# A retention recurrence and a multiplicative FFN on one core: w3 @ w_out multiplied once on the chip, the recurrence done chunk by chunk for all heads with head pairs padded to the full array, in a fixed instruction order

## The chip, the core and the metric

The kernel runs on one core of one Trainium2 chip. The metric is the device time of one execution in microseconds (us). Where a median is quoted it is that of the runs of one session; the kernel before was run beside every kernel of this study, in the same session and on the same chip as it (the sessions had different chips), and stayed at 430.7 to 433.3 us as a median. Engines are named as in the profile: PE is TensorE, PEld its weight loads, DVE is VectorE, ACT is ScalarE, POOL is GpSimd, SP is the engine that issues the DMAs here.

## The reference, cut to what matters

```python
# q, k, v: (4 batches, 8 heads, 768 steps, 64), float32
for t in range(S):
    state = gamma[h] * state + outer(k[:, :, t], v[:, :, t])
    y[:, :, t] = (1 / sqrt(D)) * (q[:, :, t] @ state)
x = y as (3072 tokens, 512)
a = x @ w1                  # 512 x 1024
b = x @ w2                  # 512 x 1024
h = (a * b) @ w3            # 1024 x 1024
return h @ w_out            # 1024 x 512
```

Two facts of it carry the change. Nothing stands between `@ w3` and `@ w_out`, so the two can be one matrix of 1024 x 512. And the decays `gamma` differ only by head, so chunks of 128 steps of all eight heads can be treated alike.

## The kernel before

Both kernels use the chunked form of the recurrence: within a chunk of 128 steps, masked scores times V; between chunks, a 64 x 64 state per head. All matmuls are in float16 with float32 sums. The kernel before takes one head of one batch after another. Its unit of work is one chunk of one head, and each unit uses the array in four shapes:

```python
def run_head(b, h, ffn_rate):            # for 32 heads, 6 chunks each
    for c in range(NCH + 2):             # three stages, one chunk apart
        # stage 3: YS[0:64] = V^T ATm + S^T tq ; K^T V for the state
        nc.tensor.matmul(YS[0:64], lhsT=V16[...], rhs=st["atm"], ...)          # 128*64
        nc.tensor.matmul(YS[0:64], lhsT=prev, rhs=st["tq"], ...)               # 64*64
        nc.tensor.matmul(YS[64:128, 0:64], lhsT=QgK[...], rhs=V16[...], ...)   # 128*64
        ...                              # copies to XT, new state, scaled state
        # stage 2: scores and mask
        nc.tensor.matmul(ATps, lhsT=st["tk"], rhs=st["tq"], ...)               # 64*128
        nc.vector.tensor_tensor(ATm, ATps, MASKT[h], MULT)
        # stage 1: one transpose of [q k]
        nc.tensor.transpose(Tps, QgK[...], ident16)                            # 128*128
        ...                              # copies tq (ScalarE), tk (VectorE)
        slot_filler()                    # pulls FFN units at a set rate
```

The FFN is a generator whose units are pulled between chunk steps. A tile of 512 tokens has 8 units of w1, 8 of w2 (four 512-column matmuls each), then the third layer, then 4 output units:

```python
for gb in range(8):
    psG = ps_g.tile([128, TB], FP, tag="psG")
    for f1b in range(8):
        nc.tensor.matmul(psG, lhsT=W3[f1b][:, gb*128:(gb+1)*128], rhs=HT[f1b], ...)
    gt = fsb.tile([128, TB], HP, tag=f"gt{gb}")
    nc.scalar.copy(gt, psG)
    yield
...
gpb = 28
quota = {0: 0, 1: 1 * gpb, 2: 3 * gpb, 3: 4 * gpb}   # FFN units to be done by the end of batch b
```

Of the kernel before, what the change touches and what calls it, by code (L numbers as in the profile page):

```python
# [9 lines left out]
FP = mybir.dt.float32  # L10
# [3 lines left out]
ADD = mybir.AluOpType.add  # L14


@with_exitstack
def kernel(
# [14 lines left out]
    NCH = S // C  # L33
    NTOK = B * S
    DM = 512
    DFF = 1024
    scale = 1.0 / math.sqrt(D)
# [3 lines left out]
    wstage = ctx.enter_context(tc.tile_pool(name="wstage", bufs=4))  # L41
    xpool = ctx.enter_context(tc.tile_pool(name="xpool", bufs=1))
    rsb = ctx.enter_context(tc.tile_pool(name="rsb", bufs=4))
    tpool = ctx.enter_context(tc.tile_pool(name="tpool", bufs=3))
    spool = ctx.enter_context(tc.tile_pool(name="spool", bufs=4))
    fsb = ctx.enter_context(tc.tile_pool(name="fsb", bufs=2))

    ps_r = ctx.enter_context(tc.tile_pool(name="ps_r", bufs=3, space=bass.MemoryType.PSUM))
    ps_a = ctx.enter_context(tc.tile_pool(name="ps_a", bufs=1, space=bass.MemoryType.PSUM))
    ps_b = ctx.enter_context(tc.tile_pool(name="ps_b", bufs=1, space=bass.MemoryType.PSUM))  # L50
    ps_g = ctx.enter_context(tc.tile_pool(name="ps_g", bufs=2, space=bass.MemoryType.PSUM))
    ps_o = ctx.enter_context(tc.tile_pool(name="ps_o", bufs=1, space=bass.MemoryType.PSUM))

    XT = [xpool.tile([128, NTOK], HP, name=f"xt{fb}") for fb in range(4)]

    heads = [(b, h) for b in range(B) for h in range(H)]

    def head_dma(b, h):
        QK = rsb.tile([128, NCH * 128], FP, tag=f"qk")
        V6 = rsb.tile([128, NCH * 64], FP, tag=f"v6")  # L60
        qk_view = QK[:, :].rearrange("p (c x) -> p c x", x=128)
        nc.sync.dma_start(
            qk_view[:, :, 0:64], q[b, h].rearrange("(c i) d -> i c d", c=NCH)
        )
        nc.sync.dma_start(
            qk_view[:, :, 64:128], k[b, h].rearrange("(c i) d -> i c d", c=NCH)
        )
        nc.sync.dma_start(
            V6[:, :].rearrange("p (c d) -> p c d", d=64),
            v[b, h].rearrange("(c i) d -> i c d", c=NCH),  # L70
        )
        return QK, V6

    dma_tiles = {}
    for h in range(H):
        dma_tiles[(0, h)] = head_dma(0, h)
# [4 lines left out]
    nc.scalar.copy(ident16[:, :], ident[:, :])  # L81

    iota64 = const.tile([128, 64], mybir.dt.int32, name="iota64")
    nc.gpsimd.iota(iota64[:, :], pattern=[[0, 64]], base=0, channel_multiplier=1)
    iotaf = const.tile([128, 64], FP, name="iotaf")
    nc.vector.tensor_copy(iotaf[:, :], iota64[:, :])

    SC = []
    MASKT = []
    GC = []  # L90
    for h in range(H):
        g = 1.0 - 2.0 ** (-5.0 - h)
        lg = math.log(g)
        sc_h = const.tile([128, 128], FP, name=f"sc{h}")
        bq = const.tile([128, 1], FP, name=f"bq{h}")
        nc.gpsimd.memset(bq[:, :], lg + math.log(scale))
        bk = const.tile([128, 1], FP, name=f"bk{h}")
        nc.gpsimd.memset(bk[:, :], (C - 1) * lg)
        nc.scalar.activation(sc_h[:, 0:64], iotaf[:, :], AF.Exp, bias=bq, scale=lg)
        nc.scalar.activation(sc_h[:, 64:128], iotaf[:, :], AF.Exp, bias=bk, scale=-lg)  # L100
        maskt_h = const.tile([128, 128], FP, name=f"maskt{h}")
        make_upper_triangular(nc, maskt_h[:, :], val=g ** (-C), diag=True)
        SC.append(sc_h)
        MASKT.append(maskt_h)
        GC.append(g**C)

    def load_weights(w_ap, nblk, ncol, name):
        tiles = []
        for i in range(nblk):
            stg = wstage.tile([128, ncol], FP, tag="wst", name=f"stg_{name}{i}")  # L110
            nc.sync.dma_start(stg[:, :], w_ap[i * 128 : (i + 1) * 128, :])
            w16 = wpool.tile([128, ncol], HP, name=f"{name}{i}")
            if i % 2 == 0:
                nc.vector.tensor_copy(w16[:, :], stg[:, :])  # L114
            else:
                nc.scalar.copy(w16[:, :], stg[:, :])  # L116
            tiles.append(w16)
        return tiles

    W1 = load_weights(moe_w1, 4, DFF, "w1")  # L120
    W2 = load_weights(moe_w2, 4, DFF, "w2")
    W3 = load_weights(moe_w3, 8, DFF, "w3")
    WO = load_weights(moe_w_out, 8, DM, "wo")

    TB = 512
    NTB = NTOK // TB

    def ffn_gen():
        pending = []

        def out_stage(tok0, GT):
            def run(tb):
                psO = ps_o.tile([128, DM], FP, tag="psO")
                for gb in range(8):
                    nc.tensor.matmul(  # L135
                        psO[:, :],
                        lhsT=GT[gb][:, tb * 128 : (tb + 1) * 128],
                        rhs=WO[gb][:, :],
                        start=(gb == 0),
                        stop=(gb == 7),  # L140
                    )
                osb = fsb.tile([128, DM], FP, tag="osb")
                nc.scalar.copy(osb[:, :], psO[:, :])  # L143
                nc.sync.dma_start(
                    out[tok0 + tb * 128 : tok0 + (tb + 1) * 128, :], osb[:, :]
                )
            return [(run, tb) for tb in range(TB // 128)]

        for t in range(NTB):
            tok0 = t * TB  # L150
            HT = []
            for f1b in range(8):
                psA = ps_a.tile([128, TB], FP, tag="psA")
                for fb in range(4):
                    nc.tensor.matmul(  # L155
                        psA[:, :],
                        lhsT=W1[fb][:, f1b * 128 : (f1b + 1) * 128],
                        rhs=XT[fb][:, tok0 : tok0 + TB],
                        start=(fb == 0),
                        stop=(fb == 3),  # L160
                    )
                pa = fsb.tile([128, TB], FP, tag="pa")
                nc.scalar.copy(pa[:, :], psA[:, :])  # L163
                yield
                psB = ps_b.tile([128, TB], FP, tag="psB")
                for fb in range(4):
                    nc.tensor.matmul(  # L167
                        psB[:, :],
                        lhsT=W2[fb][:, f1b * 128 : (f1b + 1) * 128],
                        rhs=XT[fb][:, tok0 : tok0 + TB],  # L170
                        start=(fb == 0),
                        stop=(fb == 3),
                    )
                ht = fsb.tile([128, TB], HP, tag=f"ht{f1b}", name=f"ht{t%2}_{f1b}")
                nc.vector.tensor_tensor(ht[:, :], pa[:, :], psB[:, :], MULT)  # L175
                HT.append(ht)
                yield
                if pending and f1b % 2 == 1:
                    fn, tb = pending.pop(0)
                    fn(tb)  # L180
                    yield
            GT = []
            for gb in range(8):
                psG = ps_g.tile([128, TB], FP, tag="psG")
                for f1b in range(8):
                    nc.tensor.matmul(  # L186
                        psG[:, :],
                        lhsT=W3[f1b][:, gb * 128 : (gb + 1) * 128],
                        rhs=HT[f1b][:, :],
                        start=(f1b == 0),  # L190
                        stop=(f1b == 7),
                    )
                gt = fsb.tile([128, TB], HP, tag=f"gt{gb}", name=f"gt{t%2}_{gb}")
                nc.scalar.copy(gt[:, :], psG[:, :])  # L194
                GT.append(gt)
                yield
                if pending and gb % 2 == 1:
                    fn, tb = pending.pop(0)
                    fn(tb)
                    yield  # L200
            while pending:
                fn, tb = pending.pop(0)
                fn(tb)
                yield
            pending = out_stage(tok0, GT)
        while pending:
            fn, tb = pending.pop(0)
            fn(tb)
            yield

    fgen = ffn_gen()
    ffn_done = [False]

    def pull_ffn(n):
        for _ in range(n):
            if ffn_done[0]:
                return
            try:
                next(fgen)
            except StopIteration:  # L220
                ffn_done[0] = True
                return

# [116 lines left out]
    while not ffn_done[0]:  # L340
        pull_ffn(1)
# [30 lines left out]
```

## Time and profile before

| | |
|---|---|
| time, median (range) | 431.19 us (430.96 to 431.57), 4 runs |
| profiled span | 429.0 us |
| PE busy | 392.2 us, 1888 matmuls and transposes |
| of these, third layer of the FFN | 384 matmuls |
| DVE / ACT / POOL busy | 216.4 / 175.2 / 36.0 us |

The page's rows of costliest groups give the line, engine, operation, tiles, shape and count; then the busy time in us and the mean of one instruction in ns; then the idle time ahead of them. The largest row is the third FFN layer:

```profile
L186 PE MATMUL psG<-ht,w 128*128 128x512 f16 x384 | 100.1, 381 | 0.0
```

The mean of 381 ns in this row is how long one matmul is in the pipe, and it overlaps with its neighbours. What a matmul costs TensorE is the distance from its start to the next start, 0.216 us for these. I use that distance throughout, and it is read from the timeline. The lines that show what bounds this kernel stand in the prediction.

### The profile page before, as it was taken

The numbers are of one execution on the slowest core, as the hardware profiler recorded it, in microseconds if no ns is written. First come the engines' busy times: TensorE is split into PE (matmuls) and PEld (weight loads), VectorE is DVE, ScalarE is ACT, GpSimd is POOL, SyncE is SP. The second block draws the span as 40 slices with busy tenths as digits, with TensorE's granted clock in tenths as the row PEclk, the third lists the DMA queues.
The fourth block names the chain that finished last, engine by engine and source line by source line (L and its number), as shares of the span: only waits on it lengthen the run. The fifth ranks groups of instructions, "written<-read, shape, count | busy, mean of one in ns | idle before, by whom it ended". The sixth has DMA issues, their size and how long they took to land.

```text
span 429.0 us, 6007 instructions
## 1 busy us (share of the span) xinstructions
PE 392.2 (91%) x1888; PEld 173.0 (40%) x1888; DVE 216.4 (50%) x829; ACT 175.2 (41%) x534; POOL 36.0 (8%) x71
## 2 busy tenths in 40 slices
PE   0677877799999989999999999999999999999995
PEld 0333333334444433444444444444444444444442
DVE  2666766658755565675565642566654453012100
ACT  5234465433444433444444334444444343233331
POOL 5211000010011120111111110111010000000000
PEclk9999999999999986999999999999999999999999
DMA  8971886795422342222223320201000001001102
GB/s 185 220 232 51 240 256 200 180 192 126 96 55 57 90 121 55 55 57 55 57 56 104 82 77 4 57 26 44 30 2 0 3 24 49 26 0 50 49 0 99
DMA packets 82209, 36.05 MB, mean 84 GB/s; under 512 B 76033, under 2 KB 76033, under 8 KB 82177
## 3 DMA queue, kind: packets, MB, share of 16 engines
q1 hardware_dynamic: 82176, 35.66, 32.7%
q8 instruction: 15, 0.25, 0.3%
q14 instruction: 18, 0.14, 0.1%
HBM read 29.36 MB, written 6.29 MB: 83 GB/s over the span
## 4 chain that ended last, share of the span: by engine, by line
PE 87%; DVE 5%; ACT 3%; issue 2%; DMA 2%; SPq 1%; DVEq 0%; ACTq 0%
PE psG L186 21%; PE psB L167 12%; PE psA L155 11%; PE psO L135 10%; PE R L264 8%; PE R L272 7%; PE R L306 7%; PE R L279 6%; PE R L321 5%; DVE ATm L314 2%; DMA stg_wo<-in_moe_w_out_dram 1%; DMA QK<-in_k_dram 1%; DVE S_new L292 1%; ACT osb L143 1%; ACT xt L286 1%
## 5 line engine op out<-in xcount | busy, mean ns | idle before, releaser
L186 PE MATMUL psG<-ht,w 128*128 128x512 f16 x384 | 100.1, 381 | 0.0
L286 ACT CAST xt<-R 64x128 f16<-64x128 f32 x192 | 49.5, 258 | 117.6 <-PE R L279 111.3
L314 DVE TENSOR_TENSOR ATm<-R,maskt 128x128 f16<-128x128 f32 x192 | 55.5, 291 | 73.5 <-PE R L306 70.0
L167 PE MATMUL psB<-xt,w 128*128 128x512 f16 x192 | 62.2, 395 | 0.2 <-ACT w L116 0.2
L326 ACT COPY tq<-R 64x128 f16<-64x128 f16 x192 | 48.8, 259 | 32.9 <-PE R L321 30.1
L155 PE MATMUL psA<-xt,w 128*128 128x512 f16 x192 | 58.5, 398 | 0.8 <-DVE w L114 0.5
L264 PE MATMUL R<-ATm,V 128*64 128x128 f16 x192 | 48.1, 253 | 10.0 <-DVE ATm L314 9.1
L321 PE MATMUL R<-ident,QgK 128*128 128x128 f16 x192 | 45.1, 242 | 11.6 <-DVE QgK L231 6.5
L229 POOL CAST V<-V 128x384 f16<-128x384 f32 x32 | 31.5, 984 | 277.9 <-PE R L279 229.3
L175 DVE TENSOR_TENSOR ht<-pa,psB 128x512 f16<-128x512 f32 x48 | 33.0, 687 | 43.0 <-PE psB L167 42.1
L135 PE MATMUL psO<-wo,gt 128*128 128x512 f16 x192 | 51.0, 380 | 2.4 <-ACT osb L143 2.3
L292 DVE TENSOR_TENSOR S_new<-R,ssc 64x64 f16<-64x64 f32 x160 | 36.1, 225 | 31.3 <-ACT xt L286 27.5
L306 PE MATMUL R<-tq,tk 64*128 64x128 f16 x192 | 45.0, 243 | 6.0 <-DVE tk L327 4.7
L327 DVE COPY tk<-R 64x128 f16<-64x128 f16 x192 | 42.1, 224 | 11.4 <-ACT tq L326 8.6
L186 PEld LDWEIGHTS <-w 128*128 128x128 f16 x384 | 33.6, 98 | 32.6
L194 ACT CAST gt<-psG 128x512 f16<-128x512 f32 x48 | 28.0, 585 | 39.3 <-PE psG L186 39.0
L264 PEld LDWEIGHTS <-V 128*64 128x64 f16 x192 | 21.3, 112 | 55.7 <-issue 47.3
L272 PE MATMUL R<-tq,S_new 64*64 64x128 f16 x160 | 41.6, 260 | 2.3 <-DVE S_new L292 0.8
L279 PE MATMUL R<-V,QgK 128*64 128x64 f16 x192 | 43.6, 229 | 0.0
L231 DVE TENSOR_TENSOR QgK<-QK,sc 128x768 f16<-128x768 f32 x32 | 30.5, 954 | 20.7 <-PE R L279 14.0
L163 ACT COPY pa<-psA 128x512 f32<-128x512 f32 x48 | 28.1, 585 | 30.2 <-PE psA L155 29.1
L272 PEld LDWEIGHTS <-S_new 64*64 64x64 f16 x160 | 17.4, 109 | 42.6 <-DVE S_new L292 15.4
(29 smaller groups left out, 189.8 us busy)
## 6 DMA issues: line engine op xcount, KB each, us to landing
stg_w<-in_moe_w_dram SPq DMA_DIRECT2D x16, 512.0 KB, 4.2
QK<-in_q_dram SPq DMA_DIRECT2D x32, 192.0 KB, 3.3
QK<-in_k_dram SPq DMA_DIRECT2D x32, 192.0 KB, 3.7
V<-in_v_dram SPq DMA_DIRECT2D x32, 192.0 KB, 3.4
out_dram<-osb SPq DMA_DIRECT2D x24, 256.0 KB, 2.0
stg_wo<-in_moe_w_out_dram SPq DMA_DIRECT2D x8, 256.0 KB, 2.8
```

The lines of the kernel that those rows point to most:

```text
L135: nc.tensor.matmul(psO[:, :], lhsT=GT[gb][:, tb * 128 : (tb + 1) * 128], rhs=WO[gb][:, :], start=(gb == 0), stop=(gb == 7),)
L155: nc.tensor.matmul(psA[:, :], lhsT=W1[fb][:, f1b * 128 : (f1b + 1) * 128], rhs=XT[fb][:, tok0 : tok0 + TB], start=(fb == 0), stop=(fb == 3),)
L167: nc.tensor.matmul(psB[:, :], lhsT=W2[fb][:, f1b * 128 : (f1b + 1) * 128], rhs=XT[fb][:, tok0 : tok0 + TB], start=(fb == 0), stop=(fb == 3),)
L186: nc.tensor.matmul(psG[:, :], lhsT=W3[f1b][:, gb * 128 : (gb + 1) * 128], rhs=HT[f1b][:, :], start=(f1b == 0), stop=(f1b == 7),)
L264: nc.tensor.matmul(YS[0:64], lhsT=V16[:, c3 * 64 : (c3 + 1) * 64], rhs=st["atm"][:, :], start=True, stop=(prev is None),)
L272: nc.tensor.matmul(YS[0:64], lhsT=prev[:, :], rhs=st["tq"][:, :], start=False, stop=True,)
L279: nc.tensor.matmul(YS[64:128, 0:64], lhsT=QgK[:, c3 * 128 + 64 : (c3 + 1) * 128], rhs=V16[:, c3 * 64 : (c3 + 1) * 64], start=True, stop=True,)
L286: nc.scalar.copy(XT[fb][r0 : r0 + 64, col0 + c3 * 128 : col0 + (c3 + 1) * 128], YS[0:64],)
L306: nc.tensor.matmul(ATps, lhsT=st["tk"][:, :], rhs=st["tq"][:, :], start=True, stop=True,)
L314: nc.vector.tensor_tensor(ATm[:, :], ATps, MASKT[h][:, :], MULT)
L321: nc.tensor.transpose(Tps, QgK[:, c * 128 : (c + 1) * 128], ident16[:, :])
L326: nc.scalar.copy(tq[:, :], Tps[0:64])
```

## The change

It has three parts. First, `w3 @ w_out` is multiplied once on the chip, which removes the third layer. Second, the recurrence takes one chunk of all 8 heads at a time. Two heads share the 128 rows of the array: q and V of the pair stand in tiles with zeros in the other head's half, so every matmul is 128*128. Third, the framework's scheduler is switched off (`manual_schedule`): each engine's instructions run in the order in which the program writes them. Intent: less work for TensorE, no changes of array shape, and few large instructions on the other engines.

```diff
+    ctx.enter_context(tc.manual_schedule())
...
+    def w3_transpose(f):                 # W3[f]: 128 rows of w3
+        ps = ps_t.tile([128, 1024], HP, tag="psT", name="psT")
+        for g in range(8):
+            nc.tensor.transpose(ps[:, g*128:(g+1)*128], W3[f][:, g*128:(g+1)*128], ident16[:, :])
+        t = att.tile([128, 1024], HP, tag="w3t", name="w3t")
+        nc.vector.tensor_copy(t[:, :], ps[:, :])
+    def w3_mm(f):
+        for g in range(8):
+            nc.tensor.matmul(ps[:, :], lhsT=t[:, g*128:(g+1)*128], rhs=WO[g][:, :], ...)
+        nc.scalar.copy(W3O[f][:, :], ps[:, :])
+    w3_transpose(0)
+    for f in range(8):
+        if f + 1 < 8:
+            w3_transpose(f + 1)
+        w3_mm(f)
...
+    def transposes(n):      # 4 of q, 4 of k; copies kT, qT (VectorE), qp twice (ScalarE)
+    def scores(n):          # 4 matmuls of 256 columns: lhsT=kT pair, rhs=qp padded; mask x2
+    def kv(n):              # 4 matmuls K^T V; state sum (VectorE) and its scaling (GpSimd)
+    def outputs(n):
+        for p in range(NP):
+            nc.tensor.matmul(ps[:, p, :], lhsT=vp[:, p, 0, :], rhs=am[:, p, 0, :], ...)
+            nc.tensor.matmul(ps[:, p, :], lhsT=vp[:, p, 1, :], rhs=am[:, p, 1, :], ...)
+            if c > 0:
+                nc.tensor.matmul(ps[:, p, :], lhsT=Tst[0][:, p, :], rhs=qT[:, p, :], ...)
...
-            for gb in range(8):          # the third layer, see above
...
+    for n in range(NSTEP):               # 24 steps
+        load_chunk(n + PRE)
+        ...                              # m FFN units for this step, in four parts
+        casts(n + 2)
+        transposes(n + 1)
+        pull(parts[0])
+        scores(n)
+        pull(parts[1])
+        t_new = kv(n)
+        pull(parts[2])
+        outputs(n)
+        pull(parts[3])
```

All weights go through six staging buffers. The loads are issued in this order: w_out and w3, chunks 0 and 1, w1 and w2, the other chunks.

## The prediction

> **What bounds the kernel now.** I read the page's head and its chain of waits first, then stretches of the span cut by stage, then the order of matmuls inside the longest stage.
>
> ```profile
> span 429.0 us, 6007 instructions
> PE 392.2 (91%) x1888; PEld 173.0 (40%) x1888; DVE 216.4 (50%) x829; ACT 175.2 (41%) x534; POOL 36.0 (8%) x71
> ...
> PE 87%; DVE 5%; ACT 3%; issue 2%; DMA 2%; SPq 1%; DVEq 0%; ACTq 0%
> ```
>
> TensorE holds 87% of the chain that ends last; VectorE and ScalarE are half idle. The stretches (span, then busy time with instructions of PE, PEld, DVE, ACT, POOL, then granted clock, DMA share, GB/s) show three stages:
>
> ```profile
> 0.00:83.00 83.00, 54.52 (x234) 25.80 (x235) 50.10 (x200) 38.39 (x124) 11.11 (x47) 1.00 0.74 195
> 83.00:90.00 7.00, 6.75 (x19) 1.84 (x18) 3.38 (x12) 2.20 (x6) 1.52 (x3) 1.00 1.20 219
> 90.00:360.00 270.00, 267.65 (x1351) 117.44 (x1351) 155.40 (x608) 113.57 (x368) 23.35 (x21) 0.98 0.24 58
> 360.00:429.00 69.00, 63.31 (x288) 27.95 (x286) 7.55 (x11) 21.06 (x36) 0.00 (x0) 0.99 0.10 39
> ```
>
> Up to 83 us almost only batch 0's recurrence runs; from 90 to 360 us recurrence and FFN are mixed; the rest is FFN alone. In the FFN-alone stretch, groups of four 512-column matmuls start at 385.97, 386.84 and 387.70 us: (387.70 - 385.97) / 8, one per 0.216 us. The same stretches for the recurrence's PSUM tile alone:
>
> ```profile
> 90.00:360.00 270.00, 126.86 (x693) 0.98 0.24 58
> ```
>
> The other 658 matmuls there are FFN ones: 658 x 0.216 = 142 us. That leaves 270 - 142 = 128 us for 693 small matmuls, 0.185 us each, although they stream only 64 or 128 columns (128/512 of 0.216 is 0.054). The timeline shows why (start, duration, line, shape; `128*64` is the part of the array used):
>
> ```profile
> 245.10 0.24 PE L264 MATMUL R<-ATm,V 128*64 128x128 f16 x1
> 245.27 0.24 PE L272 MATMUL R<-tq,S_new 64*64 64x128 f16 x1
> 245.44 0.22 PE L279 MATMUL R<-V,QgK 128*64 128x64 f16 x1
> 245.59 0.23 PE L306 MATMUL R<-tq,tk 64*128 64x128 f16 x1
> 245.75 0.23 PE L321 MATMUL R<-ident,QgK 128*128 128x128 f16 x1
> 245.82 1.03 PE L155 MATMUL psA<-xt,w 128*128 128x512 f16 x4
> 246.68 0.22 PE L321 MATMUL R<-ident,QgK 128*128 128x128 f16 x1
> 246.74 0.38 PE L167 MATMUL psB<-xt,w 128*128 128x512 f16 x1
> ```
>
> Wherever the shape of the array changes, start to start is 0.15 to 0.17 us. Where a 128*128 transpose is followed by a 128*128 matmul it is 0.06 to 0.07 us. So the loss is in switching shapes.
>
> **What the Trainium skill says.** TensorEngine Tiling (Array Packing), Key Properties: changing the tiling mode, not just the tile, drains TensorE. The lines above agree: 0.15 to 0.17 against 0.06 to 0.07 us.
> TensorE: Matmul & The Clock Gate, Part 1: the array runs at half rate until it has been busy for some 3.4 us. The trace agrees in the durations, though its granted clock says 1.00 there: three matmuls at 85.58 us take 1.46 us, a 512-column one 0.63, so (1.46 - 0.63) / 2 = 0.415 us apart; after 90 us it is 0.216. Thin recurrence work at 80% "busy" did not wake the clock in 80 us; dense FFN did in about 7.
> VectorE: DVE Perf Modes, Why PSUM operands drop a tier: fp32 from PSUM runs at one element a cycle, 16-bit at up to two. The rows agree:
>
> ```profile
> L314 DVE TENSOR_TENSOR ATm<-R,maskt 128x128 f16<-128x128 f32 x192 | 55.5, 291 | 73.5 <-PE R L306 70.0
> L175 DVE TENSOR_TENSOR ht<-pa,psB 128x512 f16<-128x512 f32 x48 | 33.0, 687 | 43.0 <-PE psB L167 42.1
> L327 DVE COPY tk<-R 64x128 f16<-64x128 f16 x192 | 42.1, 224 | 11.4 <-ACT tq L326 8.6
> ```
>
> (687 - 291) / 384 is 1.03 ns an element with 159 ns fixed; the f16 copy is then 159 plus 0.51 ns an element.
> SBUF — State Buffer, Who interferes with whom: a VectorE instruction with two SBUF inputs locks out GpSimd, one with a PSUM input doesn't. The cast of V on GpSimd takes 0.51 us alone and 1.24 us in most runs beside the QgK multiply (for example at 120.3 us), which agrees. The new VectorE work of the steady stage all has a PSUM input, so I count GpSimd at its quick rate.
>
> **The change, part by part.** (1) FFN: the third matmul layer goes: 384 of 960 wide matmuls, 384 x 0.216 = 83 us of TensorE. Added: 64 wide matmuls and 64 transposes for w3 @ w_out, 64 x 0.216 + 64 x 0.065 = 18 us warm; they run in the load phase, where TensorE has nothing else. ScalarE loses 48 evictions of 585 ns (28 us) and has 8 new ones.
> (2) Recurrence: 24 chunk steps for all heads, each with 8 transposes, 4 score matmuls of 256 columns, 4 K^T V ones and 8 to 12 output ones; the last chunk of a batch and the first need 4 fewer. In all 544 of 128 columns and 96 of 256, all on 128*128: 544 x 0.065 + 96 x 0.108 = 46 us, 1.9 us a step, against 693 x 0.185 = 128 us in the mixed stage plus the latency-bound 70 us of batch 0 before it. The padding multiplies zeros, but drains nothing.
> (3) The other engines, per step, from the rates above. VectorE: two f16 copies at 0.42, and masks (two), state sum and output scaling at 0.69: 3.6 us, and two ht at 0.69 with FFN: 5.0. ScalarE (585 ns for 512 columns, 258 for 128; 0.62 for a cast from SBUF): 0.62 + 2 x 0.585, two pa and one output eviction: 3.5 us. GpSimd: a cast of 512 at about 0.65 and three two-input multiplies, my estimate 2.7 in sum: 3.4 us. All are under TensorE's 5.2 + 1.9 = 7.1 us.
>
> Now the sum by stage. **Start.** The weights now come first, 6.3 MB of w_out and w3, then 2 chunks, then w1 and w2. The rates are in 2 us stretches of before (last column GB/s), rows of 256 B first, rows of 4 KB second:
>
> ```profile
> 20.00:22.00 2.00, 1.18 (x7) 0.62 (x6) 1.79 (x6) 0.84 (x4) 1.18 (x1) 1.00 1.27 219
> ...
> 24.00:26.00 2.00, 1.62 (x8) 0.78 (x7) 0.75 (x4) 0.77 (x3) 0.00 (x0) 1.00 1.03 406
> ```
>
> Six staging buffers; the first are freed by ScalarE after 16 exponentials (about 8 us), so a bubble comes there and w3 lands by about 21 us (4.5 MB after 10 us at 406). TensorE starts the product at 15 us when the second w3 tile is cast: one round of 8 + 8 cold is 8 x 0.43 + 8 x 0.11 = 4.3 us, seven warm ones 8 x 0.216 + 0.5 and waits = 2.4 us: the product ends near 37 us and is bound by TensorE, not by DMA. Only then do the casts of w1 and w2 run (they stand behind the product in the fixed order), and the last two w2 loads wait for those casts: w2 done near 43 us. Chunks 2, 3, 4 are issued behind w2, 0.79 MB each at 219 GB/s = 3.6 us: 44.5, 48, 52 us. ScalarE's cast of chunk n + 2 stands at the head of step n, so steps 0 and 1 crawl and step 2, the first with FFN, starts at about 54 us.
> **Steps 2 to 23.** FFN per step at 0.216: steps 2 and 3 3.5 us, 4 to 7 2.6, 8 to 11 4.3, 12 to 23 5.2. With 1.9 for the recurrence, and VectorE's 4.4 to 5.3 us and the handovers as the limit of the early ones: 2 x 6.3 + 4 x 5.8 + 4 x 6.6 + 12 x 7.5 = 152 us. I went through one full step by hand: the masked scores are ready about when the outputs want them, and the three shared PSUM banks come free in time, so I expect short waits only.
> **Tail.** The last 512 tokens cannot start before step 23: 64 + 32 + 32 wide matmuls x 0.216 = 27.6 us, then the eviction and the output DMA, 3 us (before: last eviction ends at 426.1, span 429.0): 31 us.
> 54 + 152 + 31 = 237 us. Time over span is 431.39 - 429.0 = 2.4; for waits of the in-order queues, and the first steps at half rate, I add 4 to 5% of the 200 us from the first step on, 8.6: 248 us. Without the 8.6 it is 239.
>
> **Rivals.** (a) *The engines wait for one another in the fixed order*, VectorE first: at 5.0 of 7.5 us it is two thirds busy, and each late mask or ht stops TensorE. Against it: FFN units stand between every two recurrence stages. If a step took 8.7 us throughout, 22 x 8.7 = 191 instead of 152: 287 us less part of my allowance, some 280.
> (b) *The start takes more.* If the product stays at half rate, it ends at 15 + 8 x 4.3 = 50 instead of 37 us: 261 us. For it: 80 us of cold clock in before; against it: this work is dense.
> (c) *Small matmuls keep costing 0.185 us*, because the reason is weights or semaphores rather than array shapes: 640 x 0.185 = 118 instead of 46 us, about 315 us. The 0.06 to 0.07 us after 128*128 transposes speak against it.
> (d) *GpSimd becomes the bound*, if strided and broadcast inputs triple its multiplies: 0.65 + 8 = 9 us a step, about 280 us. Nothing in the trace shows a two-input GpSimd instruction, so this is open.
>
> **Range and chances.** The lower end is no waits and a start 5 us shorter, 234; the upper end takes most of (a), (b) or (d) alone, 278. Even (c) is 27% faster than before, so faster is nearly sure; the small rest is for a stall I don't see.
>
> **What would show it.** Right: TensorE's product of w3 between about 15 and 37 us with idle TensorE up to about 45; groups of 128-column matmuls 0.06 to 0.09 us apart; steps of 7 to 8 us between 120 and 210 us with TensorE over 90% busy and the chain mostly on TensorE; a tail of 31 us. Wrong: 0.15 us or more between full-array matmuls (c), long idle of TensorE released by VectorE masks (a), wide matmuls at 0.43 us past 30 us (b), or TensorE waiting for GpSimd's k, v or state tiles (d).

## The result, and the profile after

Median 236.56 us (235.65 to 236.82, 4 runs) against 431.19 us. The ratio is 0.5479, with a 95% interval of 0.5463 to 0.5495. Ratios here are the mean time of one kernel's fast runs over the mean of the other's fast runs of the same rounds, so not quite the ratio of the medians quoted. Executions over 1.5% slower than the fastest of the same kernel are left out of the means. The predicted 248 us was 11 us too high, inside its range; the sum of stages without the allowance was 239.

The head of the page after, with the chain of waits:

```profile
span 234.7 us, 3859 instructions
PE 194.7 (83%) x1408; PEld 116.2 (49%) x1408; DVE 120.0 (51%) x225; ACT 105.5 (45%) x193; POOL 67.7 (29%) x102
...
PE 63%; DVE 14%; ACT 8%; DMA 7%; issue 5%; SPq 1%; DVEq 0%; ACTq 0%
```

TensorE's busy time was halved, from 392 to 195 us. VectorE's instructions fell from 829 to 225. TensorE's share of the chain fell from 87% to 63%, though, and VectorE's rose from 5% to 14%. So there is waiting in the new kernel, and the stretches say where (columns as in the prediction: span, then PE, PEld, DVE, ACT, POOL, then granted clock, DMA share and GB/s):

```profile
12.00:40.00 28.00, 15.80 (x106) 8.88 (x107) 7.00 (x11) 9.46 (x13) 3.59 (x6) 1.00 0.93 309
40.00:60.00 20.00, 13.10 (x100) 9.31 (x98) 10.91 (x21) 12.58 (x20) 6.28 (x10) 0.74 1.01 217
...
90.00:203.00 113.00, 110.44 (x799) 63.22 (x797) 70.92 (x128) 51.82 (x92) 39.37 (x54) 1.00 0.52 113
203.00:234.70 31.70, 28.07 (x131) 12.53 (x128) 5.50 (x8) 10.05 (x17) 0.00 (x0) 1.00 0.20 75
```

From 12 to 60 us TensorE is busy 29 of 48 us. From 90 us on it is nearly full. The tail, 203 to 234.7, is 31.7 us.

**The steady steps.** Part of one step on the timeline of TensorE after (start, duration, line, shape, count):

```profile
142.38 1.02 PE L291 MATMUL psFB<-xt,w 128*128 128x512 f16 x4
143.32 0.22 PE L267 MATMUL psY<-am,vp 128*128 128x128 f16 x1
143.38 0.22 PE L268 MATMUL psY<-am,vp 128*128 128x128 f16 x1
143.44 0.22 PE L270 MATMUL psY<-qT,t 128*128 128x128 f16 x1
...
143.60 0.22 PE L270 MATMUL psY<-qT,t 128*128 128x128 f16 x1
143.92 0.22 PE L267 MATMUL psY<-am,vp 128*128 128x128 f16 x1
```

Two things are to be seen. The full-array 128-column matmuls start every 0.055 us, where the mixed shapes before took 0.15 to 0.17. And twice there is a gap: 142.38 + 4 x 0.216 = 143.24, but the first output matmul starts at 143.32; and from 143.60 to 143.92 there is 0.32 us where 0.055 would do. The gaps, 0.08 + 0.26 = 0.34 us, fall at the two halves of the masked scores. VectorE at that moment:

```profile
141.99 0.69 DVE L296 TENSOR_TENSOR ht<-pa,psFB 128x512 f16<-128x512 f32 x1 [1.90 <-ACT pa L287]
142.59 1.28 DVE L232 TENSOR_TENSOR am<-psA,keep 128x512 f16<-128x512 f32 x2
```

The scores were done by TensorE at about 141.4, but the `ht` product of the FFN stood ahead of the masks in VectorE's fixed order, and it had itself waited 1.90 us for ScalarE's `pa`. The two masks end at 143.87, 5 hundredths before the second half of the outputs starts. Full steps are 7.30 us long: 24 wide matmuls x 0.2165 = 5.20, small ones (24 x 0.055 + 4 x 0.11) = 1.76, and 0.34 of waiting.

**The start.** TensorE up to the first product rounds:

```profile
9.44 1.04 PE L154 MATMUL psT<-ident,w 128*128 128x128 f16 x8 [9.44 <-DVE w L135]
24.20 1.01 PE L154 MATMUL psT<-ident,w 128*128 128x128 f16 x8 [13.73 <-DVE w3t L158]
25.01 3.47 PE L165 MATMUL psW<-wo,w3t 128*128 128x512 f16 x8
```

and VectorE just before, and last one earlier line of ScalarE, the cast of w3 tile 1:

```profile
22.86 0.69 DVE L144 CAST w<-stg 128x1024 f16<-128x1024 f32 x1 [1.91 <-DMA stg<-in_moe_w_dram]
23.47 0.68 DVE L158 COPY w3t<-psT 128x1024 f16<-128x1024 f16 x1
...
16.38 1.04 ACT L146 CAST w<-stg 128x1024 f16<-128x1024 f32 x1 [0.86 <-DMA stg<-in_moe_w_dram]
```

The first transposes were done at about 10.5 us. The copy that takes them out of PSUM runs only at 23.47, because it stands behind the casts of w3 tiles 2, 4 and 6 in VectorE's order, and each of those waits for its load. TensorE stands idle for 13.73 us, but not all of it for this copy. The second transposes also need w3 tile 1, whose cast waits for its load and ends at 17.42. So some 7 us of the idle time belong to the load and cast of tile 1 and to the order that puts its transposes ahead of the first product round. The other 24.20 - 17.42 = 6.8 us belong to an instruction of 0.68 us that was ready all along. The product then runs to 43.2 us, and the first recurrence transposes, at 46.33, wait 3.08 us for ScalarE's cast of q behind two casts of w1.

### The profile page after: what moved, and what is told of

Same layout as the page of the kernel before. It is cut to its first block, busy times and chain, and to the rows that moved or that the text cites. A ratio compares the mean times of both kernels' runs of the same rounds, so it can differ in the third digit from the quotient of the medians.

```text
span 234.7 us, 3859 instructions
## 1 busy us (share of the span) xinstructions
PE 194.7 (83%) x1408; PEld 116.2 (49%) x1408; DVE 120.0 (51%) x225; ACT 105.5 (45%) x193; POOL 67.7 (29%) x102
## 4 chain that ended last, share of the span: by engine, by line
PE 63%; DVE 14%; ACT 8%; DMA 7%; issue 5%; SPq 1%; DVEq 0%; ACTq 0%
PE psO L303 18%; PE psFA L282 14%; PE psFB L291 10%; DVE am L232 8%; PE psW L165 7%; DMA stg<-in_moe_w_dram 5%; ACT qp L219 3%; PE psY L267 3%; ACT pa L287 2%; PE psA L229 2%; PE psT L210 2%; PE psT L212 2%; DMA stg<-in_moe_w_out_dram 2%; DVE ht L296 2%; PE psT L154 2%
## 5 line engine op out<-in xcount | busy, mean ns | idle before, releaser
L296 DVE TENSOR_TENSOR ht<-pa,psFB 128x512 f16<-128x512 f32 (+1 forms) x56 | 34.0, 607 | 51.6 <-ACT pa L287 33.3
L291 PE MATMUL psFB<-xt,w 128*128 128x512 f16 (+1 forms) x224 | 50.7, 349 | 2.6 <-ACT pa L287 2.5
L282 PE MATMUL psFA<-xt,w 128*128 128x512 f16 (+1 forms) x224 | 50.7, 349 | 0.9 <-DVE xt L271 0.9
L303 PE MATMUL psO<-w3o,ht 128*128 128x512 f16 x192 | 44.7, 380 | 0.0
L259 POOL TENSOR_TENSOR t<-s,GS 128x512 f16<-128x512 f32 x16 | 20.4, 1272 | 65.6 <-DVE s L258 57.1
L287 ACT COPY pa<-psFA 128x512 f32<-128x512 f32 (+1 forms) x56 | 28.8, 525 | 19.1 <-PE psFA L282 18.6
L196 POOL TENSOR_TENSOR vp<-v,VS 128x256 f16<-128x256 f32 x48 | 28.5, 615 | 13.6 <-PE psY L270 8.6
L232 DVE TENSOR_TENSOR am<-psA,keep 128x512 f16<-128x512 f32 x48 | 30.8, 682 | 0.4 <-PE psA L229 0.3
L303 PEld LDWEIGHTS <-ht 128*128 128x128 f16 x192 | 18.1, 98 | 18.9
L267 PE MATMUL psY<-am,vp 128*128 128x128 f16 x96 | 18.0, 221 | 3.9 <-DVE am L232 2.1
L268 PE MATMUL psY<-am,vp 128*128 128x128 f16 x96 | 18.1, 223 | 0.0
```

The lines of the kernel that those rows point to most:

```text
L196: nc.gpsimd.tensor_tensor(vp[:, :, r, r * 64 : r * 64 + 64], v32[:, :].rearrange("j (p s e) -> j p s e", s=2, e=64)[:, :, r, :], VS[:, :]. ...
L232: nc.vector.tensor_tensor(am[:, half * 2 : half * 2 + 2, :, :].rearrange("j p s i -> j (p s) i"), ps[:, :, :, :].rearrange("j p s i -> j ( ...
L259: nc.gpsimd.tensor_tensor(t16[:, :, :], s32[:, :, :], GS[:, :, :], MULT)
L267: nc.tensor.matmul(ps[:, p, :], lhsT=vp[:, p, 0, :], rhs=am[:, p, 0, :], start=True, stop=False)
L268: nc.tensor.matmul(ps[:, p, :], lhsT=vp[:, p, 1, :], rhs=am[:, p, 1, :], start=False, stop=(c == 0))
L282: nc.tensor.matmul(psA[:, :], lhsT=W1[d][:, f * 128 : (f + 1) * 128], rhs=XT[:, d, tok0 : tok0 + TB], start=(d == 0), stop=(d == 3),)
```

## The experiments

Twelve kernels were run; each edit is against the kernel after unless I say otherwise. All results were correct.

### One part at a time

**Only the FFN part, in the kernel before** (the product of w3 and w_out after the weights are loaded, no third layer, the output units read the product, and 20 instead of 28 FFN units a batch):

```diff
+    for f in range(8):  # 8 transposes, copy, 8 matmuls with WO, copy to W3O[f]
...
-            for gb in range(8): ...      # the third layer
-    gpb = 28
+    gpb = 20
```

> The old kernel with the FFN part of the change alone: w3 @ w_out multiplied once, third matmul layer gone, recurrence as before. Theory (the parts add up on TensorE): 384 wide matmuls of 0.216 us go (83 us) and 64 wide ones and 64 transposes come (18 us warm), which can only start when the last weights are loaded at about 82 us, so they are not hidden: 431 - 83 + 18 = 366 us, 350 to 375. Rival (without the wide matmuls between them the small ones only wait longer on one another): less than half of the gain, over 390 us.

Measured: 391.79 us (391.36 to 396.75), ratio 0.9075 [0.9008, 0.9141]. The third layer's 83 us of TensorE time, less 18 for the product, brought only 39. So the reckoning "matmuls removed times 0.216" fails in the kernel before, and a stretch in its last batch tells why. Before, then this run (columns as above):

```profile
300.00:345.00 45.00, 45.00 (x232) 20.06 (x231) 23.76 (x107) 19.03 (x66) 1.74 (x2) 1.00 0.03 11
```

```profile
300.00:345.00 45.00, 38.49 (x170) 17.57 (x170) 24.00 (x112) 16.85 (x61) 1.24 (x1) 0.66 0.03 12
```

The same view restricted to the recurrence's PSUM tile counts 133 recurrence matmuls before and 138 in this run. With 99 or with 32 wide matmuls beside them, the recurrence went on at the same pace. Its work at full clock would be 32 x 0.216 + 138 x 0.185 = 32 us of these 45. Where no FFN unit is drawn for a while, one chunk of one head follows the other like this (timeline of TensorE in this run):

```profile
311.31 0.26 PE L264 MATMUL R<-ATm,V 128*64 128x128 f16 x1 [0.38 <-DVE ATm L314]
...
312.22 0.28 PE L306 MATMUL R<-tq,tk 64*128 64x128 f16 x1
312.89 0.26 PE L264 MATMUL R<-ATm,V 128*64 128x128 f16 x1 [0.38 <-DVE ATm L314]
```

That is 1.58 us from one chunk to the next, with a wait in each on the way from scores over the mask to the outputs. The third layer had filled this wait. Taking it out left holes, and the granted clock fell to 0.66 in this stretch. The holes came first: the last wide matmul before them starts at 305.7, and the granted clock is still 1.00 from 305 to 310 us and 0.50 from 315 us on. But the lines shown are at the low clock, and part of their 1.58 us is the clock itself: from the start of L264 to that of L306 it is 0.91 us here and 0.65 at 287.08 us, where the granted clock is full.

**The same, FFN units drawn four at a time.** The low clock could be cause or consequence. If it is the cause, denser blocks of wide matmuls should keep it up:

```diff
-        budget = [0.0]
+        budget = carry            # carried over from head to head
...
-            if n > 0:
+            if n > 3:
```

> The old kernel with the FFN part alone once more, but its FFN units drawn four at a time instead of one at a time. In that run 26 us more than computed were left, the granted clock fell to 0.66 to 0.84 in three stretches, and there the recurrence ran with few wide matmuls between. Theory A (the clock is what was lost: thin work lets it fall): dense blocks of some 16 wide matmuls keep it up, mean clock over 0.95 instead of 0.903, and the time falls to 365 to 380 us. Theory B (the chain of one head, five matmuls and a mask, 1.58 us a chunk, is the bound wherever there is too little FFN work to fill it, and the low clock follows from the idle array): blocks fill the chain no better, 388 us or more.

Measured: 396.36 us (392.19 to 397.38), ratio 0.9155 [0.9101, 0.921]. The time did not fall, as theory B had it. But the blocks did not keep the clock up either: its mean was 0.891 to 0.904 in the four runs, against 0.903 to 0.904. So this run does not tell apart what the slow clock costs and what the unfilled chain costs. The trace above shows both at work, and that the holes came before the low clock; the split of the missing 26 us stays open.

**Only the recurrence part** (the kernel after, its fixed order included, with the third layer kept and no product):

```diff
-    w3_transpose(0); for f in range(8): ... w3_mm(f)
+        def g_unit(g):            # as the third layer before, units drawn like the others
```

> The new kernel with the third matmul layer kept and no product of weights: the recurrence part of the change alone. Theory: 83 us of wide matmuls come back on a TensorE that is the bound, the product's 19 us leave a start that then waits for loads instead and gets some 4 us shorter, and the idle TensorE of the first steps takes little of it: 236.6 + 83 - 5 = 315 us, 303 to 320. Rival (the new kernel's steps have much slack on TensorE): under 295 us.

Measured: 306.55 us (305.79 to 307.68), ratio 0.7085 [0.7044, 0.7127], as expected. One part alone is worth 39 us and the other 125, 164 together, while the change is worth 195: the parts don't add. The 125 us contain whatever the fixed order costs, and no run separates in them the constant shape from taking eight heads at once. On top of the new recurrence the FFN part brings 306.55 - 236.56 = 70 us instead of 39. There TensorE is the bound: from 90 to 250 us it was busy all 160 of 160 us. Most of the 83 us saved come through; against them stands a recurrence that starts later because of the product (first transposes at 46.33 instead of 37.42 us).

### The array shape

**The same outputs without the padding**: each head's V as 64 columns, writing its own 64 rows of PSUM; the state stays at the full array.

```diff
-  nc.tensor.matmul(ps[:, p, :], lhsT=vp[:, p, 0, :], rhs=am[:, p, 0, :], ...)
-  nc.tensor.matmul(ps[:, p, :], lhsT=vp[:, p, 1, :], rhs=am[:, p, 1, :], ...)
+  nc.tensor.matmul(ps[0:64, p, :], lhsT=vp[:, p, 0, 0:64], rhs=am[:, p, 0, :], ...)
+  nc.tensor.matmul(ps[64:128, p, :], lhsT=vp[:, p, 1, 64:128], rhs=am[:, p, 1, :], ...)
```

> The new kernel with the two output matmuls of each head pair given their 64 used columns only (128*64 array shape, two halves), the state matmul still 128*128: the same count and the same columns streamed, but up to 8 changes of array shape a step. Theory (changing the shape drains the array, 0.15 to 0.17 instead of 0.055 us): 168 changes of 0.1 us, 17 us where TensorE is the bound, so 247 to 254 us, and the output matmuls 0.15 us apart in the trace. Rival (the small matmuls were slow for their weight loads or semaphores): no change, 234 to 238 us.

Measured: 244.05 us (242.59 to 245.2), ratio 0.5635 [0.5601, 0.5668]: slower by 7.5 us, less than the 10 to 17 expected. The timeline of TensorE shows each term:

```profile
140.51 0.24 PE L267 MATMUL psY<-am,vp 128*64 128x128 f16 x1
140.51 0.24 PE L268 MATMUL psY<-am,vp 128*64 128x128 f16 x1
140.69 0.23 PE L270 MATMUL psY<-qT,t 128*128 128x128 f16 x1
140.85 0.24 PE L267 MATMUL psY<-am,vp 128*64 128x128 f16 x1
```

The two half-width matmuls start together, so they do run side by side in the array. But after each change of shape the next start is 0.16 to 0.18 us later, and a head pair takes 140.85 - 140.51 = 0.34 us, against 3 x 0.055 = 0.165 padded. Half the multiplications of the padded form are with zeros, and still it is twice as quick. Four pairs lose 0.7 us a step; the step grew only from 7.30 to 7.64, because nearly all of the 0.34 us of waiting is swallowed by the slower outputs (0.7 - 0.34 = 0.36). What the 0.16 us consist of the trace doesn't settle: at a change of shape the weight load starts together with its matmul (both at 140.69), while without one it starts ahead (in the kernel after: load 143.33, matmul 143.38). And this run changes the shape for every head pair. All narrow matmuls first and all state matmuls then would change it twice a step instead of eight times; that was not tried, so the run shows the price of changing and not of the narrow shape.

### The fixed order

**Without the fixed order**: one line removed, so that the framework's scheduler orders the same instructions.

```diff
-    ctx.enter_context(tc.manual_schedule())
```

> The new kernel with the line that fixes the instruction order taken out: the scheduler orders each engine's instructions itself. Theory (TensorE is the bound and its waits are only 0.3 us a step, so order matters little): within 3%, 230 to 244 us. Rival (the fixed order is what keeps TensorE fed, or it is what makes the start slow): over 5% away, either side.

Measured: 222.42 us (221.91 to 222.85), ratio 0.5136 [0.5112, 0.5161]. My expectation failed: the fixed order costs 14 us, and without it the kernel is the best of all that I ran, 6% under the change as given. TensorE in this run, start and steady part:

```profile
9.10 1.01 PE L153 MATMUL psT<-ident,w 128*128 128x128 f16 x8 [9.10 <-DVE ident L83]
10.89 2.32 PE L164 MATMUL psW<-wo,w3t 128*128 128x512 f16 x5 [0.79 <-DVE w3t L157]
...
34.69 0.39 PE L209 MATMUL psT<-ident,q 128*128 128x128 f16 x4
...
127.02 0.39 PE L209 MATMUL psT<-ident,q 128*128 128x128 f16 x4
...
133.98 0.39 PE L209 MATMUL psT<-ident,q 128*128 128x128 f16 x4
```

The product starts at 10.89 instead of 25.01 us and the recurrence at 34.69 instead of 46.33. A full step takes 133.98 - 127.02 = 6.96 us, and 5.20 + 1.76 = 6.96 is TensorE's own work: no wait is left. In that step the matmuls have the same order on TensorE as after; only VectorE's masks came in time, because the scheduler put the first of the two ahead of `ht` and the second behind it.

I then tried to get the same with the fixed order kept, place by place.

**Each w3 cast just ahead of its transposes**, so that the first copy no longer stands behind three casts:

```diff
-    for i in range(1, 8): ...                  # all casts of w3, then the product
     for f in range(8):
         if f + 1 < 8:
+            w3_cast(f + 1)
             w3_transpose(f + 1)
```

> The new kernel, fixed order kept, with each cast of a w3 tile written just ahead of its transposes instead of all casts ahead of the first transpose. In the new kernel the second group of transposes waits 13.7 us for the first copy of w3t, which stands in VectorE's order behind the casts of three later w3 tiles. Theory (this place in the order costs the start): the product starts near 17.5 instead of 24.2 us, and the time falls by 4 to 7 us, to 230 to 233 us. Rival (the start is bound by its loads whatever the order): no change, 235 to 238 us.

Measured: 234.67 us (232.44 to 235.06), ratio 0.5445 [0.5416, 0.5474], about 2 us instead of the 4 to 7 expected. The product did start early (16.25 us, once tile 1 was cast), but now every second round waits 1.62 us for a cast by ScalarE that stands behind that engine's eviction of the round before; the recurrence starts at 42.39. (The profile is of the fastest of the four runs, 232.44; with the same start in the run with both orders below it is 45.54.) Moving one instruction up in a fixed order puts others behind it.

**Scores ahead of the first FFN units of a step**, so that the masks come before `ht` in VectorE's order:

```diff
-        pull(parts[0])
         scores(n)
+        pull(parts[0])
```

> The new kernel, fixed order kept, with the scores of a step ahead of the first FFN units instead of behind them, so that VectorE masks before it multiplies the first ht. Theory (the waits of TensorE for the masks, 0.3 us in a full step and about 1 us in steps 4 to 8, come from VectorE's order: mask behind ht behind pa behind the two qp copies): full steps of 7.0 instead of 7.3 us, 5 to 9 us less in all, 228 to 232 us. Rival (the waits move to the next thing, the PSUM banks of the FFN units or the copies for the next scores): 234 to 238 us.

Measured: 229.15 us (225.97 to 229.99), ratio 0.5284 [0.5243, 0.5325]: as expected by the median, 7 us less, and 9 less by the mean. Two of the four runs, the profiled one among them, are left out of the ratio. The steps can be read from the profiles of the next two runs, which contain this edit: 6.95 to 6.96 us. From the first FFN matmul to the last transposes of q these take 181.54 - 56.79 = 124.75 and 182.70 - 57.93 = 124.77 us, the change itself 189.69 - 57.97 = 131.7: scores-first is worth 7 us in the steps. TensorE in the first of them:

```profile
56.79 0.60 PE L283 MATMUL psFA<-xt,w 128*128 128x256 f16 x4
...
181.54 0.39 PE L211 MATMUL psT<-ident,q 128*128 128x128 f16 x4
```

**Both of these**, and then a third one added (each cast two rounds ahead, and each round's matmuls ahead of the next transposes):

> Both changes of order at once (casts in the loop, scores first), order still fixed. Theory (these two places are what the scheduler's own order gained, 14 us): the gains add, 222 to 227 us, about the time without a fixed order. Rival (the scheduler gains elsewhere, by interleaving inside the steps): over 229 us.

> The fixed order with scores first and the w3 casts two tiles ahead of their transposes, and the first 8 product matmuls ahead of the second transposes, as the scheduler had placed them. With casts just one ahead every second round of the product still waited 1.6 us for ScalarE's cast behind its eviction. Theory (these places in the order are what the run without a fixed order gained): the product ends near 35 instead of 42 us, 221 to 225 us. Rival (the scheduler gains by interleaving inside the steps): 227 to 229 us as with the two orders.

Measured: 228.08 us (227.54 to 228.51), ratio 0.5302 [0.5285, 0.5318], and 228.67 us (227.97 to 229.35), ratio 0.5292 [0.5273, 0.5312]. Neither theory's range was met (the second run fell where its rival said), and neither is better than scores-first alone. In the first, TensorE waited until 18.02 us for the second w3 tile's cast and 1.62 us in every second round; in the other, the product began at 11.26 but each round waited 0.79 us for the copy of its own transposes, 3.13 us a round instead of 2.17. In both, the recurrence still started at 45.5, behind ScalarE's casts of w1. The gain of the earlier product was lost in the next place of the order.

**The scheduler's places at the start, written out in a fixed order.** I took where each instruction of the start stood in the run without the fixed order: exponentials ahead of the last four casts of w_out; first product round ahead of the second transposes; chunks 0 and 1 cast inside the product; each cast of w1 and w2 beside the first two chunk steps; chunk 2 cast only after the first FFN units. Scores first as well.

```diff
+    w3_cast(1); w3_transpose(0); w3_mm(0); w3_cast(2); w3_transpose(1)
+    for f in range(1, 8):
+        ...                         # w3_cast(f+2), w3_transpose(f+1), w3_mm(f)
+        if f == 5: casts(0)
+        if f == 6: casts(1)
+    transposes(0)
...                                  # w1 and w2 casts spread over steps 0 and 1
+        elif n == 2:
+            pull(parts[0]); casts(2); transposes(2)
```

> Fixed order again, but with every instruction of the start put where the run without the fixed order had it: exponentials ahead of the last four w_out casts, first product round ahead of the second tile's transposes, W3 casts two rounds ahead, q, k and v of chunks 0 and 1 cast inside the product, each w1 and w2 cast beside the recurrence of chunks 0 and 1 instead of ahead of it, chunk 2 cast only after the first FFN units; scores ahead of the first FFN units. Theory: it is the places alone that made the run without a fixed order quick, so they do the same in a fixed order: first product matmul near 11 us, product over near 35, first recurrence transposes near 35 (after the change 46.3), first FFN matmul near 44 (57), full steps 6.95: 220 to 225 us. Rival: the places at the start shift the waits into steps 2 to 11, or the gain lay in the interleaving inside the steps: 226 to 230 us, as my other fixed orders.

Measured: 227.37 us (225.09 to 229.01), the two fast runs 226.10 and 225.09; over the mean of the eight fast runs of before, 432.3, that is 0.522. The median falls under the rival, and the fast runs lie at the border of the two ranges, so the time does not decide. The trace does, part by part, and the first half of the theory holds to the microsecond: product from 11.26 us, first recurrence transposes at 33.28, first FFN matmul at 44.08, full steps 6.95. But in the early steps TensorE waits three times where I had placed transposes and scores too close together:

```profile
49.25 0.60 PE L224 MATMUL psA<-qp,kT 128*128 128x256 f16 x4 [2.14 <-ACT qp L214]
...
56.35 0.60 PE L224 MATMUL psA<-qp,kT 128*128 128x256 f16 x4 [2.10 <-ACT qp L214]
...
66.19 0.40 PE L205 MATMUL psT<-ident,q 128*128 128x128 f16 x4 [2.75 <-ACT q L181]
```

Those are 7.0 us: the waits had moved into the steps, as the rival said. From the first FFN matmul to the last transposes of q, this kernel takes 179.36 - 44.08 = 135.3 us, the one without a fixed order 175.27 - 44.33 = 130.9, the change itself 189.69 - 57.97 = 131.7. So the 14 us of the scheduler are accounted for: about 13.6 from an earlier start and 0.8 in all the steps after it. The mark is not quite the same point of the work: by its first FFN matmul the change has transposed four chunks, the other two kernels two, and 16 transposes at 0.055 are 0.9 us. The 0.8 is a net: 0.35 us in each full step is a gain, and the scheduler's early steps, up to 90 us, must give part of it back. What they lose it to is not separated. But the record shows that there is something to win: scores-first took 124.8 us for this stretch, 6 less than the scheduler. An order with the scheduler's start and those steps would, by my estimate from these stretches, save about 5 us more than the scheduler does, if the loads allow it (in the run without the fixed order the DMA share is 1.04 to 1.22 from 40 to 80 us). The run just shown was meant to be that and wasn't, and no other tried it.

### Another order of loads

The start is bound by loads and casts, so I also tried to begin with the recurrence and put the product later, both without the fixed order: chunk 0, w1, chunk 1, w2 first and the product after steps 2 and 3; and, after that had missed, seven chunks first and the product after steps 4 and 5.

```diff
+    load_chunk(0); casts(0); transposes(0)
+    load_w(moe_w1, W1); load_chunk(1); casts(1); load_w(moe_w2, W2)
...
+        if n == 2: w3_product(range(0, 4))      # second version: n == 4
+        if n == 3: w3_product(range(4, 8))      # second version: n == 5
```

> An attempt at a better version, without a fixed order: chunk 0, w1, chunk 1, w2 are loaded first, w_out and w3 behind them, and the product w3 @ w_out is written after steps 2 and 3, as filler. Theory (TensorE stood idle some 20 us in the first 50 because the recurrence waited for the product and then for the chunks): total work of TensorE 192 us plus about 15 us of start and waits and 3 us of end, 208 to 216 us. Rival (the early steps are bound by the loads of the chunks, and the 6.3 MB of w_out and w3 now stand in their way): 220 us or more.

> Second attempt at a better start, no fixed order: chunks 0 to 6 with w1 and w2 first, w_out and w3 only behind chunk 6, the product after steps 4 and 5, the first output units only from the third FFN tile on. The first attempt failed because chunk 3 stood behind the w_out loads, whose staging buffers were not free for 12 us. Theory (TensorE can be kept busy from about 20 us on, when chunks come every 3.6 us and a step with its FFN share takes 5.5): 192 us of work, less 8 done before, plus 23 + 3 + waits of 5: 211 to 218 us. Rival (early steps are bound by latency and loads in any order): 220 us or more.

Measured: 229.41 us (227.67 to 231.08), ratio 0.5346 [0.5316, 0.5376], and 232.21 us (231.18 to 235.11, the last of them slow), ratio 0.5365 [0.5337, 0.5393]. Both are slower than the plain run without the fixed order, and both expectations failed the same way. The eight loads of w_out go through staging buffers that are still full of weights whose casts wait their turn. SP issues in order, so they held it from 20.5 to 32.8 us in the first and from 36.6 to 47.8 us in the second, and what stood behind them came late: chunk 3 in the first (TensorE idle 4.12 us for the cast of its q), w3 in the second (4.31 us, and then a first product round at half rate again, 3.6 us for 8 matmuls). Both edits also gave up the transposes one round ahead: most rounds of the product waited 0.56 to 0.79 us for the copy of their own transposes, and a round took 3.13 us instead of 2.17. More staging buffers would be the next thing to try; I did not.

## Why the prediction was right or wrong

**Right in the result and in the main mechanism.** TensorE bounds the new kernel from 90 us on (110 of 113 us busy up to the tail), and the drop comes from its work: wide matmuls removed, and small ones that no longer change the array's shape. The rival (c), small matmuls that keep costing 0.185 us, is refuted by 0.055 us in the trace, and the run without padding shows that it is the shape and not the number of columns: 0.34 us a pair at 64 columns against 0.165 at 128. The 46 us for the 640 small matmuls were mis-sized: 544 x 0.055 + 96 x 0.11 = 40.5.

**Steps and tail.** From step 2's transposes at 57.0 to the end of step 23 at 203 it took 146 us where I said 152; the tail 31.7 where I said 31. Full steps were 7.30, not 7.5: the small matmuls cost 1.76 instead of 1.9, and the sum had allowed for more handover. The allowance of 8.6 us for the in-order queues and the half-rate first steps was not needed on top. So the total is 11 us off by a sum of errors with both signs: start +3, steps -6, tail +1, allowance -9.

**The step that failed is the start**: "TensorE starts the product at 15 us when the second w3 tile is cast". The tile was cast at 17.42, but TensorE also needed the PSUM buffer that VectorE's copy was to free, and that copy stood behind three casts: 24.20 us, 9 late, 2 of them for the tile and 7 for the copy. I had followed the fixed order for w1, w2 and chunk 2, and not for VectorE inside the product. That the total still came close is luck. Two errors the other way hid the late start: a warm round takes 2.17 us, not 2.4, and there was more slack before step 2 than I thought, so the product's end at 43.2 instead of 37 moved step 2 only from 54 to 57. The first round at half rate was sized right: 8 + 8 in 28.31 - 24.20 = 4.1 us, predicted 4.3.

**"The masked scores are ready about when the outputs want them"** was short by 0.34 us a step. So rival (a), the engines waiting for one another, holds in small: scores-first took the wait out, 7.30 became 6.95, and all the steps together became 7 us shorter. Rival (b) named the right stage and the wrong reason: only one round was at half rate, the rest was a late start.

**Rival (d) falls.** GpSimd's rows after:

```profile
L259 POOL TENSOR_TENSOR t<-s,GS 128x512 f16<-128x512 f32 x16 | 20.4, 1272 | 65.6 <-DVE s L258 57.1
...
L196 POOL TENSOR_TENSOR vp<-v,VS 128x256 f16<-128x256 f32 x48 | 28.5, 615 | 13.6 <-PE psY L270 8.6
```

Two multiplies of 0.615, one of 1.27 and a cast of 0.61 make 3.1 us a step, where I had estimated 3.4. Per element, the strided multiply with a broadcast input (0.615 us for 256, 2.4 ns) costs no more than the plain one (1.272 for 512, 2.5 ns).

**What the prediction took for granted** and the experiments overturned: that the FFN's 83 us and the recurrence's gain are separate terms. They add up in the new kernel, because TensorE is the bound there. In the old one the FFN was also the filler of a latency chain, and cutting it alone brought 39 us. And I counted the third part of the change only as an allowance of 8.6 us for waits. Against the run without it the fixed order costs 14 us, and nearly all of that was already in my start of 54 us, where I had followed the order without asking what another would give: the change without it is at 222.

## What to carry to other kernels

Count the changes of the array's shape, and see whether zeros can avoid them: here, where the shape changes, one start follows the other at the distance of three full-array matmuls of 128 columns (0.16 against 0.055 us). Before removing work from the busiest engine, see in each stage whether that work is the bound or the filler of somebody else's wait; if it is filler, it is worth little until the chain beneath it is shortened. And take a fixed instruction order as a claim to be tested against the scheduler's: one copy behind three casts kept TensorE idle for 7 us. One repair by hand, scores-first, took 7 us out of the steps, each repair of the start moved the wait to the next engine, and removing one line was better than all of them.

## What the Trainium skill lacked or had wrong

- TensorEngine Tiling (Array Packing), Key Properties, says that a change of tiling mode drains TensorE, and gives no size. Here it is 0.15 to 0.18 us from start to start, against 0.055 us without a change. Packing two 64-column operands beside each other, with a full-array matmul after each pair, therefore lost: 0.34 us a head pair instead of 0.165, although the two halves did start together.
- TensorE: Matmul & The Clock Gate, Back-to-back issue gap, gives a sustained spacing of some 81 ns for 128 columns and 131 ns for 512 in pairs of weight load and matmul. Here each matmul has its own weight load, and the spacing is 55 ns and 216 ns, which is what the same page calls the isolated gap.
- The same page, Part 4: PE-mode transpose, says that the full clock doesn't engage for transposes, and gives some 275 ns for one in a kernel. Here eight f16 transposes between matmuls start 0.056 us apart when warm (28.31 to 28.76 us) and 0.10 us apart when cold (24.20 to 25.01 us), so they go at full clock as matmuls do. The length of one does agree (242 ns in the mean of these rows), but it overlaps with its neighbours, so a row of them costs far less than 275 ns each. The records call them MATMUL, so the trace doesn't show whether the page's transpose mode is on, and whether transposes alone would wake the clock, no run shows.
- TensorE: Matmul & The Clock Gate, Part 1, warns that clock events in traces have been unreliable, without such a case. Here the granted clock in the records is 1.00 while matmuls run at half rate: after the change at 25 to 28 us (0.41 us a wide matmul where a warm one takes 0.216). So the durations decide and not the clock column.
